# An attention and feed-forward kernel: output product in quadrants, two head chunks in 64x32 tiles, stages from token tables

One core of one Trainium2 chip. The metric is the device time of one execution in microseconds (us), lower is better. Each "time" below is the median of the runs of a kernel; a "span" is that of the one profiled execution and is some 2 us shorter than the time. PE is TensorE and PEld its weight loads, DVE is VectorE, ACT ScalarE, POOL GpSimd; SP is SyncE, whose queue issues transfers. PSUM is the memory that matmuls write.

## The reference

For 8 batches, 12 heads, 448 tokens and head width 64: q and k are normalised by their root mean square, then softmax attention. The result, 3584 rows of 768, goes through a feed-forward layer of width 2048 with a sine in the middle.

```python
q_n, k_n = rmsnorm(q, g_q), rmsnorm(k, g_k)
scores = np.matmul(q_n, k_n.transpose(0, 1, 3, 2)) / np.sqrt(64)
attn = np.exp(scores - max); attn = attn / (sum(attn) + 1e-09)
x = np.matmul(attn, v)                  # -> (B*S, H*D) = (3584, 768)
h = x @ w_in                            # first product, 768 -> 2048
s = np.sin(alpha * h)
g = h + s * s / (alpha + 1e-09)
return g @ w_out                        # output product, 2048 -> 768
```

## The kernel before

The program is unrolled. For each batch there is a stage in which attention runs beside the output product of the batch before; then comes the first product of the batch. I call such a pair a repeat. A batch has three chunks of four heads. `bank_pair` hands out one of four pairs of PSUM banks (a slot): the one that a small clock model, run when the program is built, takes to be free first. The order within a stage comes from a short plan string, between whose entries the output steps and the side work are spaced evenly.

```python
def bank_pair(name, dtype=F32):
    slot = min(free_at, key=free_at.get)          # a modelled time at which each slot comes free
    clock["pe"] = max(clock["pe"], free_at.pop(slot))
    ...

def load_v(b):                                    # four transfers of 64 rows
    ...
    parts = [(slots[pp][key_rows(pp, hi)], tok[hi, pp]) for pp in range(2) for hi in range(2)]
    return [lambda o=o, i=i: nc.gpsimd.dma_start(out=o, in_=i) for o, i in parts]

def load_w_in(half):                              # two transfers of 64 rows a half
    rows = moe_w_in.rearrange("(hi pr d) f -> hi d pr f", hi=2, d=D)
    cols = slice(half * D_FF // 2, (half + 1) * D_FF // 2)
    for hi in range(2):
        nc.gpsimd.dma_start(out=w_in_sb[half][hi * 64:hi * 64 + 64], in_=rows[hi, :, :, cols])

def attend(pi, tiles=range(NJ)):                  # values and 64 copies of the sums, 64x64 tiles
    ...
    nc.tensor.matmul(av[o, part, :S], ones[r, :] if part else vb[b][r, hp, j, :],
                     expT[pi // 2, j][r, pi % 2, :], start=(j == 0), stop=(j == NJ - 1))
    ...

def step(m, unit=unit, st=st):                    # output product, whole array
    ...
    nc.tensor.matmul(st["ps"][:, k, :HALF], g_sb[:, m, c0:c0 + P],
                     w_out_sb[:, m, half * HALF:(half + 1) * HALF], start=(m == 0), stop=(m == MT - 1))
```

In the general stage, the four value loads of the next batch go out one at a time near the end of the attention stage, and the transposes of q and k by DMA (`transpose`, two a chunk, on the SP queue) go out early (those of the batch's own third chunk, which this stage still needs), in the middle and at the end (those of the next batch's first two chunks).

## Time and profile before

| before | |
|---|---|
| time | 436.38 us (436.36 to 437.89) |
| span of the profiled run, mean granted TensorE clock | 434.6 us, 0.996 |
| end of the first product of batch 1, then one repeat | 107.71 us, then 50.35 us each |
| after the last first product (the close) | 24.8 us |

Two more groups of lines of this page: the first lists a DMA queue (packets, MB, share of 16 engines' time); the others an issue (count, KB each, median us from issue to landing).

```profile
q0 software_dynamic: 12416, 11.81, 18.0%
...
w_in<-in_moe_w_in_dram POOLq DMA_DIRECT2D x4, 768.0 KB, 11.9
```

### The profile page before, as it was taken

What the parts mean: (1) busy time and instruction counts of PE and PEld (TensorE: products, weight loads), DVE (VectorE), ACT (ScalarE), POOL (GpSimd) and SP (SyncE); (2) the same over time, 40 slices, a digit from 0 to 9 for tenths busy, and PEclk for the clock granted to TensorE, in tenths of its full rate; (3) what the DMA queues carried; (4) which work ended last, traced back from release to release, by engine and by line L of the source; (5) the groups of instructions that cost most, each with busy time, mean ns of one, the idle gap of its engine ahead of it and who ended that gap; (6) DMA issues with size and microseconds to landing.
All of it is one profiled execution on the core that took longest, in us unless ns stands there. A gap on an engine that the chain in (4) does not pass through costs nothing.

```text
span 434.6 us, 9514 instructions
## 1 busy us (share of the span) xinstructions
PE 423.9 (98%) x3844; PEld 220.5 (51%) x3844; DVE 231.6 (53%) x335; ACT 338.4 (78%) x529; POOL 279.7 (64%) x263
## 2 busy tenths in 40 slices
PE   7889999999999999999999999999999999999996
PEld 3335554555455555555555555555555555555563
DVE  4778564557455564547453564464645474246511
ACT  4889789878888787878879788887878788788600
POOL 4969789936995659927798369947599176002300
PEclk9989999999999999999999999999999999999999
DMA  7999999690249505692067903494063901320022
GB/s 254 209 257 206 215 192 231 143 267 15 67 151 217 144 0 131 121 223 100 10 193 180 194 1 82 150 221 125 1 196 85 126 1 33 84 57 2 0 67 79
DMA packets 68240, 54.63 MB, mean 126 GB/s; under 512 B 39636, under 2 KB 63972, under 8 KB 68196
## 3 DMA queue, kind: packets, MB, share of 16 engines
q1 hardware_dynamic: 54834, 40.51, 36.1%
q0 software_dynamic: 12416, 11.81, 18.0%
q10 hardware_dynamic: 946, 1.70, 1.0%
q8 instruction: 30, 0.49, 0.5%
q14 instruction: 14, 0.11, 0.1%
HBM read 45.62 MB, written 11.01 MB: 130 GB/s over the span
## 4 chain that ended last, share of the span: by engine, by line
PE 82%; DVE 1%; ACT 1%; POOL 0%; issue 0%; POOLq 0%
PE ops L406 32%; PE hps L353 29%; PE av L314 13%; PE sc L294 7%; ACT expT L297 1%; DVE ms L227 0%; POOL sq L221 0%; DVE osb L412 0%; DVE g_sb L340 0%; DVE xT L326 0%; ACT inv L236 0%; ACT inv L237 0%; POOLq L246 0%
## 5 line engine op out<-in xcount | busy, mean ns | idle before, releaser
L297 ACT ACTIVATE expT<-sc 128x896 bf16<-128x896 f32 x168 | 144.7, 914 | 30.6 <-PE sc L294 29.5
L406 PE MATMUL ops<-w_out_sb,g_sb 128*128 128x384 bf16 x896 | 156.6, 327 | 0.0
L353 PE MATMUL hps<-xT,w_in 128*128 128x448 bf16 x768 | 146.8, 353 | 0.0
L335 POOL TENSOR_TENSOR s<-s 128x448 f32<-128x448 f32 x64 | 59.5, 934 | 114.4 <-ACT s L332 100.8
L406 PEld LDWEIGHTS <-g_sb 128*128 128x128 bf16 x896 | 83.1, 98 | 70.0 <-issue 18.8
L340 DVE SCALAR_TENSOR_TENSOR g_sb<-s,inv_alpha_sb,hps 128x448 bf16<-128x448 f32 x128 | 80.8, 676 | 60.9 <-POOL s L335 60.9
L353 PEld LDWEIGHTS <-w_in 128*128 128x128 bf16 x768 | 74.4, 98 | 71.4 <-issue 2.9
L332 ACT ACTIVATE s<-hps,alpha_sb 128x448 f32<-128x448 f32 x128 | 74.6, 628 | 28.3 <-PE hps L353 26.5
L326 DVE TENSOR_TENSOR xT<-av,rec 64x448 bf16<-64x448 f32 x96 | 59.7, 622 | 50.1 <-ACT rec L321 30.8
L246 POOL TENSOR_TENSOR qkn<-qk,inv 128x448 bf16<-128x448 f32 x80 | 72.7, 939 | 7.4 <-POOL qk L224 7.0
L221 POOL TENSOR_TENSOR sq<-qk 128x896 f32<-128x896 f32 x44 | 73.4, 1685 | 0.0
L314 PE MATMUL av<-expT,vb 64*64 64x448 bf16 x672 | 70.6, 352 | 0.6 <-DVE osb L412 0.3
L314 PE MATMUL av<-expT,ones 64*64 64x448 bf16 x672 | 70.7, 352 | 0.0
L227 DVE TENSOR_REDUCE ms<-sq 128x14 f32<-128x896 f32 x44 | 47.5, 1083 | 25.0 <-POOL sq L221 24.7
L412 DVE COPY osb<-ops 128x768 f32<-128x768 f32 (+1 forms) x33 | 27.6, 837 | 51.4 <-PE ops L406 45.5
L294 PE MATMUL sc<-qkT 64*64 64x448 bf16 x672 | 51.3, 362 | 2.5 <-DVE qkT L276 1.4
L224 POOL TENSOR_TENSOR qk<-qk,gg 128x896 f32<-128x896 f32 x24 | 50.2, 2094 | 1.8 <-ACT gg L171 1.8
L314 PEld LDWEIGHTS <-vb 64*64 64x64 bf16 x672 | 37.6, 107 | 12.5 <-issue 1.1
L314 PEld LDWEIGHTS <-ones 64*64 64x64 bf16 x672 | 37.4, 107 | 11.3
L337 ACT ACTIVATE s<-s 128x448 f32<-128x448 f32 x64 | 36.9, 577 | 2.8
L294 PEld LDWEIGHTS <-qkT 64*64 64x64 bf16 x672 | 15.1, 105 | 30.6 <-issue 26.4
L321 ACT ACTIVATE rec<-rec 128x448 f32<-128x448 f32 x48 | 27.7, 577 | 1.5
(44 smaller groups left out, 138.6 us busy)
## 6 DMA issues: line engine op xcount, KB each, us to landing
qk<-in_q_dram SPq DMA_DIRECT2D x24, 448.0 KB, 4.8
qk<-in_k_dram SPq DMA_DIRECT2D x22, 448.0 KB, 4.8
out_dram<-osb SPq DMA_DIRECT2D x39, 192.0 KB, 2.8
vb<-in_v_dram POOLq DMA_DIRECT2D x32, 168.0 KB, 6.4
w_in<-in_moe_w_in_dram POOLq DMA_DIRECT2D x4, 768.0 KB, 11.9
w_out_sb<-in_moe_w_out_dram POOLq DMA_DIRECT2D x2, 1536.0 KB, 24.2
out_dram<-osb SPq DMA_DIRECT2D x26, 96.0 KB, 4.5
qk<-in_k_dram ACTq DMA_DIRECT2D x2, 448.0 KB, 6.0
```

The source lines that it names most:

```text
L221: nc.gpsimd.tensor_mul(st.sq[w], qk[ci][:, w], qk[ci][:, w])
L224: eng.tensor_mul(qk[ci][:, 0], qk[ci][:, 0], gg.to_broadcast([P, 2 * NJ, D]))
L246: eng.tensor_mul(n[:, :, hi, :], x[:, hi], inv[:, hi].unsqueeze(2).to_broadcast([P, NJ, D]))
L294: nc.tensor.matmul(sc[key_rows(pp, hi), pp, :S], qkt[r, 1, j * REST:(j + 1) * REST], qkt[r, 0, :], start=True, stop=True)
L297: nc.scalar.activation(expT[c, j], sc[:, :, :S], ACT.Exp, scale=SCALE)
L314: nc.tensor.matmul(av[o, part, :S], ones[r, :] if part else vb[b][r, hp, j, :], expT[pi // 2, j][r, pi % 2, :], start=(j == 0), stop=(j == ...
L326: nc.vector.tensor_mul(xT[b][r, hp, :], av[r, 0, :S], rec[o, :])
L332: nc.scalar.activation(s1, hps, ACT.Sin, scale=alpha_sb[:, m, :])
L335: nc.gpsimd.tensor_mul(s2, s1, s1)
L340: nc.vector.scalar_tensor_tensor(g_sb[:, m, (b % 2) * S:(b % 2 + 1) * S], s2, inv_alpha_sb[:, m, :], hps, op0=ALU.mult, op1=ALU.add)
L353: nc.tensor.matmul(ps[:, m % 2, :S], w_in_sb[m * 2 // MT][:, kt, m % (MT // 2) * P:(m % (MT // 2) + 1) * P], x[:, kt, :], start=(kt == 0), ...
L406: nc.tensor.matmul(st["ps"][:, k, :HALF], g_sb[:, m, c0:c0 + P], w_out_sb[:, m, half * HALF:(half + 1) * HALF], start=(m == 0), stop=(m == ...
```

## The change

The intent: (1) the output product in four 64x64 quadrants a matmul, so that output, scores and values share one tile shape and TensorE changes shape less often; (2) the sums and values of two of the three head chunks together in eight 64x32 tiles, so that sums are not made twice; (3) the order of a stage written out in tables of tokens instead of spaced evenly from a short plan, with the PSUM slot of each tile named in a string instead of picked by the model. Because the heads are grouped in another way, the loads of values and of the first weights are rewritten as well. Cut to its core (the order code and the first two tables are left out; "..." marks cuts):

```diff
+STAGE_N = (
+    (
+        "r2 S 1 q40 5 f f f k20 f 1 S 3 f 1 f u40 S S f 1 k21 1 q41 q31 1 t2 S 1 V1 1 S 1 g4 1 S 2 u31 S "
+        "1 u41 S 2 S f f 1 S 2 S 2 q30 S 1 S o6 o1 v4 1 v1 u30 S v1 g3 r4 v1 f f 1 k41 2 S 1 S 1 l5 1 f "
+        "q50 S f k40 f S f 1 q51 t4 S 1 r3 1 k30 1 k31 S 1 x1 l6 x6 y4 y1 y2 z2 z2 z2 z1 "
+    ),
+    "32103020210230230310310132131313103210210",
+    {-1: 'g5 t3', 0: 'u50', 5: 'u51', 6: 'l7'},
+)
+LAST = "0123012"
...
     def bank_pair(name, dtype=F32):
-        slot = min(free_at, key=free_at.get)
-        clock["pe"] = max(clock["pe"], free_at.pop(slot))
+        slot = int(upcoming.popleft())
+        free_at.remove(slot)
...
     def load_v(b):
-        parts = [(slots[pp][key_rows(pp, hi)], tok[hi, pp]) for pp in range(2) for hi in range(2)]
-        return [lambda o=o, i=i: nc.gpsimd.dma_start(out=o, in_=i) for o, i in parts]
+        heads = v[b].rearrange("(g pp) (p j) d -> (pp p) g (j d)", pp=2, j=NJ)
+        nc.gpsimd.dma_start(out=vb[b].rearrange("p g j d -> p g (j d)"), in_=heads)
...
     def load_w_in(half):
-        rows = moe_w_in.rearrange("(hi pr d) f -> hi d pr f", hi=2, d=D)
         cols = slice(half * D_FF // 2, (half + 1) * D_FF // 2)
+        pairs = moe_w_in.rearrange("(c hi pp d) f -> c pp hi d f", c=NC, pp=2, d=D)
+        quarters = moe_w_in.rearrange("(g x d) f -> g x d f", x=2, d=D // 2)
+        for pp in range(2):
+            nc.gpsimd.dma_start(out=w_in_sb[half][:, pp], in_=pairs[0, pp, :, :, cols])
+        for x in range(2):
+            nc.gpsimd.dma_start(out=w_in_sb[half][:, 2 + x], in_=quarters[4:8, x, :, cols])
         for hi in range(2):
-            nc.gpsimd.dma_start(out=w_in_sb[half][hi * 64:hi * 64 + 64], in_=rows[hi, :, :, cols])
+            for pp in range(2):
+                g = 8 + 2 * hi + pp
+                nc.gpsimd.dma_start(out=w_in_sb[half][strip(2, pp, hi), 4:6], in_=quarters[g, :, :, cols].rearrange("x d f -> d x f"))
...
+            for hi in range(2):
+                for c in ((1, 2) if both else (0,)):
+                    for pp in range(2):
+                        r = slice(pp * 64, pp * 64 + 64)
+                        o, k = (strip(c, pp, hi), c - 1) if both else (slice(hi * 64, hi * 64 + 64), pp)
+                        d = slice(D // 2) if kind in ("ones", "low") and both else slice(D // 2, D) if both else slice(D)
+                        w = ones[r, d] if kind == "ones" else vb[b][r, 2 * c + hi, j, d]
+                        nc.tensor.matmul(av[o, k, :S], w, expT[b * NC + c, j][r, hi, :], start=(j == 0), stop=(j == NJ - 1))
...
+            def quadrants(m, unit=unit, st=st):
...
+                for r in range(2):
+                    for o in range(2):
+                        rs, os = slice(r * 64, r * 64 + 64), slice(o * 64, o * 64 + 64)
+                        nc.tensor.matmul(st["ps"][os, r, :HALF], g_sb[rs, m, c0 + o * 64:c0 + o * 64 + 64],
+                                         w_out_sb[rs, m, half * HALF:(half + 1) * HALF], start=(m == 0), stop=(m == MT - 1))
+                if m == MT - 1:
...
+                    nc.vector.tensor_copy(osb[:, 0], st["ps"][:, 0, :HALF])
+                    nc.vector.tensor_add(osb[:, 0], osb[:, 0], st["ps"][:, 1, :HALF])
...
+            step = whole_array if b == B - 1 else quadrants
```

In the tables, a number is so many output steps, S a chunk of scores, o v x y z the sums and values, t a pair of DMA transposes, V the load of values, W and O the first and the output weights; the string of digits names the slot of each PSUM tile in turn.

## The prediction

> **What bounds the kernel now.** I read the page's busy shares and the 40 slices first, then the chain that ended last in order of time over one whole repeat, then the groups by shape, the waits, and the busy time by stage.
>
> ```profile
> span 434.6 us, 9514 instructions
> PE 423.9 (98%) x3844; PEld 220.5 (51%) x3844; DVE 231.6 (53%) x335; ACT 338.4 (78%) x529; POOL 279.7 (64%) x263
> PE   7889999999999999999999999999999999999996
> DMA  7999999690249505692067903494063901320022
> ```
>
> PE is at 98%, but matmul ends are modelled and matmuls overlap, so the share alone proves little. The chain does prove it. From 81 us on it is PE alone until the last copy, and every repeat (one batch: attention beside the output product of the batch before, then the first product) takes the same 50.35 us: first product ends at 107.71, 158.06, 208.41, 258.76, 309.12, 359.47, 409.82. Inside one repeat:
>
> ```profile
> 158.06 1.95 PE ops L406 x12
> 160.01 0.50 PE sc L294 x8
> 160.51 2.38 PE ops L406 x14
> 162.89 0.50 PE sc L294 x8
> ...
> 169.87 2.71 PE ops L406 x16
> 172.57 0.50 PE sc L294 x8
> 173.07 1.32 PE av L314 x28
> 174.40 0.19 PE sc L294 x4
> 174.59 2.38 PE ops L406 x14
> ...
> 186.17 3.97 PE av L314 x84
> 190.14 18.27 PE hps L353 x96
> ...
> 409.82 20.81 PE ops L406 x128
> ```
>
> Columns: start in us, length in us, engine, tile and line, matmuls. I read unit prices out of it:
> - Whole-array output product (384 columns): the closing 128 matmuls take 20.81, or 162.6 ns each.
> - 64x64 tiles (448 columns): 84 value and sum matmuls take 3.97, or 189 ns for each four. Four quadrants truly run at once; I call four a round. A chunk of scores is one round, 0.19.
> - First product: 18.27/96 = 190 ns each, or 189 ns plus one entry of about 0.11.
> - **The price of changing tile shape.** 14 output matmuls after scores take 2.38, but 14 x 0.1626 = 2.28; 8 scores after output take 0.50, but two rounds are 0.38. So each change between 128x128 and 64x64 costs 0.10 to 0.12 us. Where the shape stays (first product to output: 12 in 1.95; scores to values: 28 in 1.32), nothing is added.
>
> The repeat from 158.06 has 18 such changes. Check of the sum: 112 output matmuls 18.21, first product 18.16, 21 scores 3.97, 42 rounds of values and sums 7.94, which is 48.28; the other 2.07 over 18 changes is 0.115 each. No part of the repeat is a wait.
>
> ```profile
> L406 PE MATMUL ops<-w_out_sb,g_sb 128*128 128x384 bf16 x896 | 156.6, 327 | 0.0
> L314 PE MATMUL av<-expT,vb 64*64 64x448 bf16 x672 | 70.6, 352 | 0.6 <-DVE osb L412 0.3
> L314 PE MATMUL av<-expT,ones 64*64 64x448 bf16 x672 | 70.7, 352 | 0.0
> ```
>
> The means of 327 and 352 ns are latencies, not prices. Half the attention product, 672 matmuls, only makes sums of the exponentials, copied to 64 rows each. ACT is busy 27.4 of the 32.1 us of the attention stage and 14.3 of 18.3 beside the first product; POOL 26.9 and 9.7; DVE 15.8 and 11.4. All have room, ACT and POOL the least.
>
> **What the Trainium skill says.**
> - "TensorEngine Tiling (Array Packing)", Key Properties: a change of tiling mode, not just of tile, drains TensorE. The trace agrees, at 0.115 us a change.
> - Same page, Available Configurations and Key Properties: 64x32 mode has eight tiles, and different tiles load weights and multiply in parallel. The trace confirms it for four 64x64 tiles (189 ns a round, eight score weight loads begun in about 35 ns); no 64x32 tile occurs in it.
> - Same page, Restrictions: column tiling turns Fast Weight Load off. In the trace a 64x64 load takes 106 ns against 98 for a full one; four together still hide under a round.
> - Same page, Gotcha 1 (PSUM Pressure): different row tiles may not be in one PSUM bank at once. Hence a quadrant product must leave two half sums in two banks, and DVE must add them. Nothing in the trace contradicts it; before never has two row tiles in the same bank and rows.
>
> **The change part by part.**
> 1. *Output product in quadrants* (all batches but the last). One matmul becomes four of 64x64. By the price of a round I expect the same 162.6 ns: no gain in arithmetic, 768 matmuls become 3072. The gain is that output, scores and values now share one shape. In the general plan the shape changes only at first product to output, into the 64x32 tiles at the end, and out of them into the first product: 3 changes for 18. That is 15 x 0.115 = 1.7 us a batch. The stage of batch 1 has 5 for 18: 1.5 us.
> 2. *Two chunks together in 64x32 tiles.* One chunk alone still takes 14 rounds (7 of sums, 7 of values). The other two took 28; now sums, low half and high half take 7 each, eight matmuls a round, because one set of sums 32 rows high serves both value halves. 42 rounds become 35: 7 x 0.189 = 1.3 us a batch, if eight tiles overlap as four do. Starts about 5 ns apart leave room for sixteen instructions inside 189 ns.
> 3. *What moves off PE.* ACT: twelve Ln and Exp a batch at 0.55 to 0.58 become four of 896 columns at about 0.9: 6.7 becomes 3.7 us. DVE: twelve products of 64x448 at 0.622 (7.5 us) become three of 128x896 at about 1.0 (3 us). But each half output row now costs a copy of 0.56 and an add I put at 0.6 (estimate: the copy of the same size): about 8 us instead of 4. DVE is about even, at 28 of 47 us. None of this is on the path; it takes ACT load off a stage that shrinks by 3 us.
> 4. *Loads.* Values come in one transfer instead of four (saves POOL about 2 us of issue a batch at 0.64 each); the first weights come in eight instead of two per half (some 4 us more POOL issue for each half, once, in the opening stage). Bytes are unchanged.
> 5. *Opening stage* (to 39.67). It also saves 7 rounds and about 3 us of ACT, but its DMA share is 0.94, POOL is 29.6 of 39.7 busy, and PE waits there for transposes and scaling. I count 1.0 us.
> 6. *Close.* The last batch's output keeps its whole-array form: the 24.8 us after 409.82 stay.
>
> **Sum.** Six repeats (batches 2 to 7) at 1.7 + 1.3 = 3.0: 18.1 us. Batch 1: 1.5 + 1.3 = 2.8, and about 0.5 of the 1.2 us of waiting that its stage has now (48.94 against 47.7 of work): 3.3. Opening: 1.0. Together 22.4 off. I give back 0.6 for new small waits on named slots and half sums. 436.4 - 22.4 + 0.6 = **414.4 us**; each repeat should read 47.3 us.
>
> **Rivals.**
> - *Eight tiles do not overlap fully.* If a 64x32 round cost 25% more (twice the instructions to place), 21 rounds x 0.047 = 1.0 us a batch: about 422. If it ran as two rounds of four, the 21 cost 4.0 us a batch more, some 32 us in eight batches, and the change would lose. For: no such tile was ever timed here. Against: load starts about 5 ns apart.
> - *The quadrants are bound by their weight loads.* A round of 384 columns is 27 ns shorter than the 448 ones whose loads are seen to hide. If a quadrant round also cost 189 ns, 112 x 0.026 = 2.9 us a batch, some 20 us over the seven batches: about 434, no gain. Against: two batches of loads, eight in all, fit into 0.14 us.
> - *ACT becomes the bound.* After the first product ends it still has 1.8 us of sines and squares, 1.28 of table load, then 21 exponentials at 0.83 back to back, 3.7 of reciprocals and 1.6 of norms: about 26 in a stage of 29. It fits, but a bad order would show as PE waiting on expT: up to 1 us a batch, about 421.
> - *The opening stays bound by transfers.* The slices show DMA at 90% and more up to about 65 us; an earlier PE then waits for weights: the 1.0 and part of batch 1 fall away, about 417.
>
> **Range and chances.** The middle rests on measured prices; what can go wrong adds time, except that the reordered opening may save 2 or 3 us instead of 1. So 410 to 420. Only a failure of concurrency, not a wait, could bring it within 2% (above 427.7): 0.95 faster, 0.04 within, 0.01 slower.
>
> **What would show each step right or wrong.** In the chain: first-product ends 47.3 us apart (46.8 to 48); scores after output at 0.19 a round with no added 0.12; output at 0.65 us for sixteen quadrant matmuls; 56 matmuls of a 64x32 part in 1.32 us. In the waits: the 80 idle gaps "issue" ahead of score weight loads (26.4 us in all) nearly gone. DVE about where it is now, ACT some 20 us lower. Wrong if output rounds read over 0.17 us, if the 64x32 parts read over 1.4 us, or if PE waits on expT, half-sum adds or weights for more than 5 us outside the first 20 us.

## More of the kernel before

The view of DMA issues over the whole run has, for the 40 transposes:

```profile
qkT<-qkn SPq DMA_TRANSPOSE x40, 4.1
```

## The result, and the profile after

The changed kernel takes **465.89 us** (464.3 to 473.32, four runs, of which the longest is slow) against 436.37 (434.85 to 437.89): the ratio is 1.0675, 95% interval 1.0631 to 1.0719. Ratios here are the mean time of one kernel's fast runs over that of the other's fast runs of the same rounds, so not quite the ratio of the medians. Without its slow run the median of the changed kernel is 465.23 us, and that of e1 459.58 for 460.72; the differences from the changed kernel given below would then be 0.7 us smaller, e1's 0.5 us larger. The kernel is 6.8% slower where I had predicted 5% faster. Its results are correct.

The page of the kernel after. The rows of digits are 40 slices of the span:

```profile
span 463.5 us, 14846 instructions
...
PE 413.9 (89%) x6598; PEld 245.6 (53%) x6598; DVE 225.8 (49%) x331; ACT 316.3 (68%) x465; POOL 275.1 (59%) x251
...
PE   4988099878996999979998999979997999999796
...
PEclk9999689998998899989999999989999999999899
...
q0 software_dynamic: 17344, 11.83, 19.0%
...
w_in<-in_moe_w_in_dram POOLq DMA_DIRECT2D x8, 256.0 KB, 16.7
w_in<-in_moe_w_in_dram POOLq DMA_DIRECT2D x8, 128.0 KB, 16.6
```

PE has 10 us less to do than before, as intended, and yet the span is 29 us longer. PE now has holes (the 0 in the fifth slice, the 6s and 7s), and the granted clock falls at the longer holes. The software queue q0 moves the same megabytes in 4,928 packets more, and the first weights land later in pieces of 256 KB than they did in pieces of 768 KB.

The chain of work that ended last, in order of time (start, length, what):

```profile
36.27 15.95 DMA w_in<-in_moe_w_in_dram
...
102.17 3.91 issue
106.09 1.30 PE av L352 x16
107.39 19.08 PE hps L392 x96
...
282.68 3.58 PE ops L471 x88
...
292.78 0.33 PE ops L471 x8
293.29 10.59 DMA qkT<-qkn
303.93 0.58 PE sc L326 x2
...
312.83 4.10 PE av L352 x168
316.92 18.27 PE hps L392 x96
...
437.04 22.46 PE ops L452 x128
```

The unit prices are the predicted ones: 88 quadrant matmuls in 3.58 us are 162.7 ns for four, and 168 of the 64x32 matmuls in 4.10 us are 195 ns for eight. But a DMA transpose of 10.59 us now stands in the chain of a repeat, a weight transfer of 16 us in the opening, and the closing product takes 22.46 us where it took 20.81. The waits say the same (total us, times, longest), first those of PE:

```profile
PE sc L326 <- DMA qkT<-qkn: 15.9, 6, 4.3
PE hps L392 <- DVE qkn L281: 12.1, 1, 12.1
PE aps L204 <- DMA small<-in_moe_alpha_dram: 6.0, 1, 6.0
PE av L352 <- issue: 4.6, 3, 3.9
PE ops L452 <- DVE g_sb L378: 3.1, 1, 3.1
```

In the profile before, the longest wait of PE with a named cause was 1.4 us in three pieces. Behind the 12.1 us stands POOL, which took its work in the order of the program:

```profile
POOL w_out_sb L227 <- DMA w_in<-in_moe_w_in_dram: 9.8, 1, 9.8
```

POOL could not issue the output weights before a first-weight transfer had landed. Behind that issue stands the product that folds in the norm's weights, then the scaling (`qkn`) on DVE, and that holds the PSUM slot which the first product was to take.

By stage, with the predicted span taken as 414.4 less the 1.8 us by which the time before exceeds its span:

| us | before | predicted | after | after less predicted |
|---|---|---|---|---|
| end of the first product of batch 1 | 107.7 | 103.4 | 126.5 | +23 |
| six repeats after it | 302.1 | 283.8 | 307.5 | +24 |
| close | 24.8 | 24.8 | 29.5 | +5 |
| span | 434.6 | 412.6 | 463.5 | +51 |

The predicted stages add up to 412.0; the rest is the 0.6 us that I gave back without a place.

### The profile page after: what moved, and what is told of

Read it like the earlier page. It is cut to its first block, busy times and chain, and to the rows that moved or that the text cites. A ratio compares the mean times of both kernels' runs of the same rounds, so it can differ in the third digit from the quotient of the medians.

```text
span 463.5 us, 14846 instructions
## 1 busy us (share of the span) xinstructions
PE 413.9 (89%) x6598; PEld 245.6 (53%) x6598; DVE 225.8 (49%) x331; ACT 316.3 (68%) x465; POOL 275.1 (59%) x251
## 4 chain that ended last, share of the span: by engine, by line
PE 71%; DMA 21%; POOL 3%; issue 2%; ACT 2%; DVE 1%; POOLq 0%; SPq 0%; ACTq 0%
PE hps L392 28%; PE ops L471 21%; DMA qkT<-qkn 14%; PE av L352 8%; PE sc L326 6%; PE ops L452 5%; DMA w_in<-in_moe_w_in_dram 3%; DMA qk<-in_k_dram 3%; PE ps L234 2%; DMA small<-in_moe_alpha_dram 1%; POOL qk L259 1%; POOL sq L256 1%; ACT s L370 1%; ACT expT L329 1%; POOL w_out_sb L227 1%
## 5 line engine op out<-in xcount | busy, mean ns | idle before, releaser
L392 PE MATMUL hps<-xT,w_in 128*128 128x448 bf16 x768 | 149.8, 356 | 13.1 <-DVE qkn L281 12.1
L471 PE MATMUL ops<-w_out_sb,g_sb 64*64 64x384 bf16 x3072 | 154.6, 329 | 0.5 <-issue 0.5
L471 PEld LDWEIGHTS <-g_sb 64*64 64x64 bf16 x3072 | 99.7, 109 | 38.4 <-issue 2.1
L326 PE MATMUL sc<-qkT 64*64 64x448 bf16 x672 | 68.5, 356 | 17.8 <-DMA qkT<-qkn 15.9
L364 DVE TENSOR_TENSOR xT<-av,rec 128x896 bf16<-128x896 f32 x24 | 25.6, 1089 | 57.0 <-PE av L352 38.9
L477 DVE COPY osb<-ops 128x384 f32<-128x384 f32 x48 | 26.7, 557 | 50.7 <-PE ops L471 50.7
L352 PE MATMUL av<-expT,vb 64*32 64x448 bf16 (+1 forms) x1120 | 41.8, 358 | 4.6 <-issue 4.6
L352 PEld LDWEIGHTS <-vb 64*32 64x32 bf16 (+1 forms) x1120 | 21.1, 97 | 16.5 <-issue 7.2
L478 DVE TENSOR_TENSOR osb<-osb,ops 128x384 f32<-128x384 f32 x48 | 26.6, 554 | 1.7
L352 PE MATMUL av<-expT,ones 64*32 64x448 bf16 (+1 forms) x672 | 25.3, 350 | 0.0
L452 PE MATMUL ops<-w_out_sb,g_sb 128*128 128x384 bf16 x128 | 22.4, 341 | 3.1 <-DVE g_sb L378 3.1
## 6 DMA issues: line engine op xcount, KB each, us to landing
w_in<-in_moe_w_in_dram POOLq DMA_DIRECT2D x8, 128.0 KB, 16.6
```

What stands on the lines that cost most here:

```text
L326: nc.tensor.matmul(sc[pp * 64:pp * 64 + 64, hi, :S], qkt[r, 1, j * REST:(j + 1) * REST], qkt[r, 0, :], start=True, stop=True)
L352: nc.tensor.matmul(av[o, k, :S], w, expT[b * NC + c, j][r, hi, :], start=(j == 0), stop=(j == NJ - 1))
L392: nc.tensor.matmul(ps[:, m % 2, :S], w_in_sb[m * 2 // MT][:, kt, m % (MT // 2) * P:(m % (MT // 2) + 1) * P], x[:, kt, :], start=(kt == ORD ...
L471: nc.tensor.matmul(st["ps"][os, r, :HALF], g_sb[rs, m, c0 + o * 64:c0 + o * 64 + 64], w_out_sb[rs, m, half * HALF:(half + 1) * HALF], star ...
```

## The experiments

Thirteen kernels ran: twelve timed, and one look after them, for what was still open. Each expectation stands as it was recorded before the run.

**e1: other closing slots.** The last eight first-product tiles take slots 0, 3, 2, 1, 0, 2, 1, 0, so the closing product, which begins with slot 0 by the table, begins with the slot that is released last.

```diff
-LAST = "0123012"
+LAST = "3210321"
```

> The changed kernel with only the closing list of PSUM slots renamed from 0123012 to 3210321, so that the first unit of the last output product takes the slot that came free first and not the one that the last snake tile still holds. Theory (named slot): the 3.1 us wait of PE on g_sb at 434 us and the half-clock stretch behind it go; the closing 128 matmuls take 20.8 us again instead of 22.5; about 4.7 us less, near 461. Rival (the last snake tile itself is late, whatever the slot): no change.

Measured 460.72 us (one of its four runs was slow), 1.055 of before [1.0499, 1.0602], so 5 us under the changed kernel. The chain shows the close as it was before:

```profile
412.56 18.27 PE hps L392 x96
430.83 20.81 PE ops L452 x128
```

The wait of 3.1 us is gone and so is the half-clock stretch that followed it. This cause is settled.

**e2: the values load later.** In the table of the general stage, `V1` follows just behind `t2`, the two transposes of the third chunk.

```diff
-... 1 t2 S 1 V1 1 S 1 g4 ...        -... k31 S 1 x1 l6 x6 ...
+... 1 t2 S 1 1 S 1 g4 ...           +... k31 S 1 V1 x1 l6 x6 ...
```

> The changed kernel with the load of the next batch's values moved from just behind the DMA transposes of the third chunk to the end of the attention stage. Theory (the 1.4 MB load slows the transposes): PE's waits on the transposes in the repeats (15.0 us) and the half-clock stretches after them go, repeats fall from 50 to 54 us to about 48, as in the last repeat, which has no such load; 10 to 19 us less, near 450. Rival (the transposes are late because scaling on POOL ends late or because the SP queue holds them): under 3 us.

Measured 441.99 us, 1.0142 [1.0117, 1.0167]: 24 us off, more than the 10 to 19 expected, and enough alone to account for the repeats. They now take 47.3 to 48.3 us. The issues of the stretch from 335 to 360 us in the kernel after, where both transposes of the third chunk and the value load fall (KB each where given, median us to landing):

```profile
vb<-in_v_dram POOLq DMA_DIRECT2D x1, 672.0 KB, 10.0
...
qkT<-qkn SPq DMA_TRANSPOSE x2, 6.7
```

The same batch's third chunk in e2 (326 to 330 us), with no value load beside it:

```profile
qkT<-qkn SPq DMA_TRANSPOSE x2, 3.4
```

PE waits for the slower of a pair: in the kernel after it was issued at 346.1 us and took 10.01 us. But e2 has only moved the load to another pair. There it runs beside the transposes of the next batch's second chunk (300 to 306 us):

```profile
vb<-in_v_dram POOLq DMA_DIRECT2D x1, 672.0 KB, 11.5
...
qkT<-qkn SPq DMA_TRANSPOSE x2, 10.3
```

These are slowed as much, and PE doesn't wait, because it needs them only 26 us after the first was issued (301.2, first use 327.2). The third chunk's pair is needed some 8 us after its issue (326.7, 334.7). In the kernel before it is the same: the transposes beside value loads take 4.7 to 8.4 us, those of the third chunk, ahead of the loads, some 3.3. So what cost the time is not that a load slows transposes, but that it was put beside the one pair that is needed soon.

The expectation was too small because it counted the waits, 15.0 us in the repeats, and too little for the clock after them: the mean granted clock from 126 to 434 us is 0.98, some 6 us in all; from 144.7 to 194.9 us it is only 0.93.

**e3: four weight transfers fewer.** The last third of the first weights goes into a tile of its own that serves both halves, 12 transfers for 16. The idea then was that the number of transfers did the harm: the program's semaphores for this queue go round in eight, so a transfer waits for the one eight places ahead of it.

```diff
+    w_last = wpool.tile([P, 2, D_FF], BF16, name="w_last")
...
+        if half:
+            return
...
-    ...out=w_in_sb[half][strip(2, pp, hi), 4:6], in_=quarters[g, :, :, cols]...
+    ...out=w_last[strip(2, pp, hi)], in_=quarters[g]...
...
```

> The changed kernel with the weights of the first product in 12 transfers instead of 16 (the rows of the last third for both halves at once). Same bytes, same place in the order. Theory (eight transfer semaphores in rotation: the first output weights wait for the first transfer of the second half to land, POOL stands still for 9.8 us, the fold behind it keeps a PSUM slot): POOL's wait ahead of the output weights goes from 9.8 to under 2 us, PE's wait of 12.1 us in the first product of batch 0 goes, the first product of batch 1 ends at 110 to 116 instead of 126 us; 10 to 16 us less. The first half is 1 MB larger, which may cost up to 4 us at its start. Rival (the bytes cannot come sooner): within 3 us of the changed kernel.

Measured 457.07 us, 1.0491 [1.044, 1.0541]: 9 us off, just under the expected range. The first product of batch 1 still ends at 120.7 us, 17 us after the predicted place, so most of the opening's loss was something else.

**e4: e1, e2 and e3 together.**

> The three edits together. If the three causes are separate, the gains add: 465.9 - 4.7 - 15 - 13, near 433, about the kernel before; repeats near 48 us. If they hide one another, the sum is clearly less than the three alone.

Measured 432.03 us, 0.9926 [0.9876, 0.9975]. From batch 2 on the predicted 47.3 us comes true, at 47.31:

```profile
99.96 18.27 PE hps L396 x96
...
147.27 18.27 PE hps L396 x96
...
194.58 18.27 PE hps L396 x96
```

Four of the six repeats take 47.31 us; the two others, 48.20 and 47.93, have each one of the halts in them that e13 is about. Over all six the granted clock is 1.00.

**e5: e4 with the whole-array output product.** This asks whether the quadrants are worth their instructions, in the order of tokens that the change has.

```diff
-            step = whole_array if b == B - 1 else quadrants
+            step = whole_array
```

> The kernel of e4 (three schedule edits) with the output product of every batch in whole 128x128 matmuls again; the order of all steps stays. In that order the tile shape then changes 42 times in a general repeat instead of 3, and 33 instead of 5 in batch 1. Theory (a change of shape costs 0.115 us): 6 x 39 x 0.115 + 28 x 0.115 = 30 us more than e4, repeats near 51.8 us. Rival (changes are hidden here, the quadrants bring nothing): within 3 us of e4; DVE is freed of the 48 adds in any case.

Measured 456.52 us, 1.05 [1.0469, 1.0531]: 24.5 us more than e4, against an expected 30. In the groups by line, the loads of weights for scores and output now wait longer without a named cause (in e4 "issue" stands at 8.2 us for scores and 1.3 for the quadrants; here busy us, mean ns, then idle us before them and what ended it):

```profile
L456 PEld LDWEIGHTS <-g_sb 128*128 128x128 bf16 x896 | 76.7, 98 | 70.8 <-issue 30.0
...
L329 PEld LDWEIGHTS <-qkT 64*64 64x64 bf16 x672 | 18.6, 103 | 48.1 <-issue 46.7
```

Each repeat has 42 changes of shape in this order for 3 with quadrants. In the profiled runs the six repeats take 312.3 us for e4's 285.4: 26.9 us over 6 x 39 = 234 changes, or 0.115 us each, the price read from the kernel before. What is missing from the 30 is in batch 1, whose repeat is 2.4 us shorter than e4's (48.3 for 50.7) where 3.2 more were expected.

**e6: the kernel before with eight weight transfers a half.** If it is the number of transfers that costs, the kernel before must suffer from it too. All have 64 rows.

```diff
-            nc.gpsimd.dma_start(out=w_in_sb[half][hi * 64:hi * 64 + 64], in_=rows[hi, :, :, cols])
+            for pr in (slice(0, 2), slice(2, 4), slice(4, 5), slice(5, 6)):
+                nc.gpsimd.dma_start(out=w_in_sb[half][hi * 64:hi * 64 + 64, pr], in_=rows[hi, :, pr, cols])
```

> The kernel before with each half of the first weights in eight transfers instead of two; same bytes, same layout, same place in the order. Theory (eight semaphores in rotation): the output weights again wait for the first transfer of the second half, POOL stands still there for 5 us or more, and the time rises by 4 to 15 us. Rival (the opening of the changed kernel is bound by other things, such as its own order): within 2 us of before.

Measured 440.43 us, 1.0134 [1.0104, 1.0164]. It is 5.5 us slower, but by another route than expected: POOL spends 6.2 us instead of 1.3 on issuing the first half (1.8 of it waiting for value loads to land), and what stands behind comes later. There is no wait ahead of the output weights, and the pieces land early, in some 8 us. The same number of transfers as in the changed kernel therefore lands in half the time. My theory of the number fell here as the main cause; what the number costs is these 5.5 us.

What differs is in the packets. In the changed kernel the trace has 5,552 packets of 4 bytes on the software queue, in e6 816, in before 624. I took it then for the form of eight of the sixteen transfers: 128 rows that lie at two strides in memory.

**e7: the kernel before with quadrants alone.**

```diff
...
+                for r in range(2):
+                    for o in range(2):
+                        rs, os = slice(r * 64, r * 64 + 64), slice(o * 64, o * 64 + 64)
+                        nc.tensor.matmul(st["ps"][os, r, :HALF], g_sb[rs, m, c0 + o * 64:c0 + o * 64 + 64], ...)
...
+                    nc.vector.tensor_copy(osb[:, 0], st["ps"][:, 0, :HALF])
+                    nc.vector.tensor_add(osb[:, 0], osb[:, 0], st["ps"][:, 1, :HALF])
```

> The kernel before with nothing changed but its output product in quadrants (all batches but the last), with half sums added on DVE. Theory: 16 of 18 changes of shape a batch go: 7 x 16 x 0.115 = 12.9 us less, near 423, repeats near 48.5 us. Rival (new waits on slots and half sums eat it): 430 or more.

Measured 434.2 us, 0.9975 [0.9954, 0.9996]. The changes of shape fall from 18 to 2 a batch as meant, but repeats fall only from 50.35 to 49.63 us, not to 48.5, and that of batch 1 grows from 48.8 to 51.8. PE now waits for DVE, which has two passes a half row and is not placed for it in this order:

```profile
PE sc L294 <- DVE osb L446: 3.9, 8, 1.4
```

These named waits are less than what is missing, and 2.5 us of them fall in batch 1; the rest wasn't followed. In this order, then, the quadrants brought little; in the order of the change (e5 against e4) they brought 24.5 us.

**e8: a first attempt at the best version.** The edits of e1 and e2, seven weight transfers a half by another assignment of strips, and a reordered opening.

```diff
...
+        for x in range(2):
+            nc.gpsimd.dma_start(out=w_in_sb[half][:96, 4 + x], in_=quarters[9:12, x, :, cols])
+        nc.gpsimd.dma_start(out=w_in_sb[half][96:, 4:6], in_=quarters[8, :, :, cols].rearrange("x d f -> d x f"))
```

> The changed kernel with the late value load and the renamed closing slots, and a mended opening: the blank matmuls first on PE, the first weights in seven transfers a half (another choice of strips), issued 2 us earlier, the fold of the next batch's first chunk ahead of them on POOL, the second half of the output weights and the values later. Theory (the opening is all that is left): POOL no longer stands ahead of the output weights; first product of batch 1 ends near 105 instead of 118 us in e4; near 418, range 414 to 424. Rival (transfers bind the opening): above 426.

Measured 432.34 us, 0.994 [0.9913, 0.9966]: a clear miss, 14 us over, in the range of the rival. Fewer transfers, and yet 7,184 packets of 4 bytes; PE waited 8.7 us for first weights. So e9 went the other way, to more transfers.

**e9: ten transfers a half, none of more than 64 rows.** With the edits of e1 and e2.

```diff
...
+        rows = moe_w_in.rearrange("(g x d) f -> g d x f", x=2, d=D // 2)
+        pairs = moe_w_in.rearrange("(c hi pp d) f -> c hi d pp f", c=NC, pp=2, d=D)
+        for hi in range(2):
+            nc.gpsimd.dma_start(out=w[hi * 64:hi * 64 + 64, 0:2], in_=pairs[0, hi, :, :, cols])
+        for c in (1, 2):
+            for hi in range(2):
+                for pp in range(2):
+                    nc.gpsimd.dma_start(out=w[strip(c, pp, hi), 2 * c:2 * c + 2], in_=rows[4 * c + 2 * hi + pp, :, :, cols])
```

> The changed kernel with the late value load and the renamed closing slots (as in e4), and the first weights in ten transfers a half, each of at most 64 rows that lie at one stride in DRAM, in place of e4's twelve in all. More transfers than in the changed kernel (8), same bytes. New theory (not the number of transfers but their form: those of 128 rows at two strides carry some 640 packets of 4 bytes each, 5120 in all, and their data starts 6 us after the issue): packets of 4 bytes fall from 5488 to about 500, the first weights land before 37 us, the first product of batch 1 ends near 112 instead of 118 us; 422 to 427. Rival (number of transfers and the eight semaphores): the opening is no better than that of the changed kernel, 436 or more.

Measured 425.23 us, 0.978 [0.9746, 0.9814], as expected (whether it is over 2% is unclear). There are 496 packets of 4 bytes, and the first product of batch 1 ends at 112.66 us.

```profile
q0 software_dynamic: 12288, 11.81, 18.6%
...
w_in<-in_moe_w_in_dram POOLq DMA_DIRECT2D x16, 128.0 KB, 7.2
w_in<-in_moe_w_in_dram POOLq DMA_DIRECT2D x4, 256.0 KB, 5.4
```

**e10: e9 with the opening's order mended.** The sines' factors no longer lead on PE, and blank matmuls keep it busy from the start; other tokens and slots of the opening moved too, as the expectation says.

```diff
-        "q01 L q00 u01 G u00 g0 r01 k01 q10 r00 b11 u10 q11 k00 b15 g1 u11 ...
+        "b11 q01 q00 u01 G u00 g0 r01 k01 q10 r00 u10 q11 k00 b15 g1 u11 ...
...
```

> e9 with the opening order mended as well: blank matmuls first on PE, the product for alpha after the first scores, the fold of the next batch's first chunk ahead of the second half of the weights, second half of the output weights and the next values inside the first product. Theory: scores start at 12 us instead of 17, the first product of batch 0 near 37 and that of batch 1 ends near 106; 413 to 420. Rival (transfers bind the opening): equal to e9 within 2 us.

Measured 423.72 us, 0.975 [0.9712, 0.9788]. The rival, no gain beyond 2 us over e9, was the nearer one: the gap at the start is closed, but the third chunk's norms now come late (PE waits 3.4 us for one transposed copy). It is the fastest of the timed kernels, 2.5% under before.

**e11: the kernel before with six transfers a half of 128 rows.** The mirror of e9: it puts the suspected form, and less of the number, into the kernel before.

```diff
-        for hi in range(2):
-            nc.gpsimd.dma_start(out=w_in_sb[half][hi * 64:hi * 64 + 64], in_=rows[hi, :, :, cols])
+        for pr in range(6):
+            nc.gpsimd.dma_start(out=w_in_sb[half][:, pr], in_=rows[:, :, pr, cols])
```

> The kernel before, with each half of the first weights in six transfers of 128 rows at two strides (one per row of tiles) in place of two of 64 rows. Theory (the form of a transfer, 128 rows at two strides, costs, not the number of transfers): each of the twelve carries 640 packets of 4 bytes, about 7,700 in all against 624 before; the weights land late, and the kernel is slower than the one with eight transfers of 64 rows a half (440.4) although it has fewer transfers: 444 us or more, with the first product of the first batch waiting for weights. Rival (each transfer costs its issue and its lane, whatever its form): six transfers cost less than eight, so 437 to 440 us and no more 4-byte packets than before.

Measured 448.84 us, 1.0323 [1.0272, 1.0375]: 14 us slower than before and 8 slower than e6, with four transfers fewer. The form costs more than the number. The lines of its page:

```profile
q0 software_dynamic: 23296, 11.85, 19.3%
...
w_in<-in_moe_w_in_dram POOLq DMA_DIRECT2D x12, 256.0 KB, 18.4
```

But there were 11,504 packets of 4 bytes and not 7,700: my 640 a transfer was wrong, and working out why gives a likely mechanism. The Trainium skill, "DMA: Bandwidth & Descriptors", section "Why a DMA increments its semaphore by 16 and not by 1", says that a transfer is spread over k of the 16 DMA engines, k being the largest number up to 16 that divides the slowest dimension (of more than one element) of both its patterns, and that on the software queue all 16 post a completion, whatever the shape. `rows[:, :, pr, cols]` begins with a dimension of two, so k is 2. Suppose that each idle engine is given one packet of 4 bytes for every row that a working engine moves, and each engine one more at the end. Then a transfer has 16 + (16 - k) x rows / k of them:

| transfer (rows, slowest dimension) | k | 4-byte packets |
|---|---|---|
| 64 rows, or 128 as one dimension | 16 | 16 |
| 128 rows as 2 x 64 (`pairs`; all of e11's) | 2 | 16 + 14 x 64 = 912 |
| 128 rows as 4 x 32 (`quarters`) | 4 | 16 + 12 x 32 = 400 |
| 96 rows as 3 x 32 (e8) | 3 | 16 + 13 x 32 = 432 |

| kernel | worked out: weights + the rest | counted in the trace |
|---|---|---|
| before | 4 x 16 + 560 | 624 |
| e6 | 16 x 16 + 560 | 816 |
| e11 | 12 x 912 + 560 | 11504 |
| e9 | 20 x 16 + 176 | 496 |
| after | 4 x 912 + 4 x 400 + 8 x 16 + 176 | 5552 |
| e8 | 4 x 912 + 4 x 400 + 4 x 432 + 2 x 16 + 176 | 7184 |

The rest is 16 for each of the 35 and 11 other transfers of this queue. The sum is right to the packet in all six (and in e3, with four transfers of 16 packets fewer: 5,488). The trace doesn't tell which engine carried a packet, so that the data went through two or four engines, and the small packets to the others, is inferred from the counts and the page's rule. By it a 256 KB transfer of the changed kernel had two or four of the sixteen engines. Whether the few engines or the small packets cost the time, no run separates. Nor does a slow transfer delay itself alone: the pieces of 128 KB at k = 16 that stand behind it in the changed kernel landed as late, after 16.6 us.

**e12: the changed kernel with e9's transfers alone.** The same test in the changed kernel.

> The changed kernel with one thing changed: each half of the first weights in ten transfers of at most 64 rows at one stride, in place of eight of which four have 128 rows at two strides. The early value load and the closing slots stay as they are. Theory (the form of these transfers is what delays the opening by some 14 us): the first product of the second batch ends at 111 to 115 instead of 126.5, its later repeats stay at 50 to 54 us each, time 450 to 454 us. Rival (the reordered opening itself, its tokens and slots, costs the time): the first product of the second batch ends at 120 or later, time 459 or more.

Measured 447.45 us, 1.0297 [1.0235, 1.0358]. The first product of batch 1 ends at 112.56 us, 14 us earlier, as expected, and its repeats keep 48 to 54 us. The time is 18.4 us under the changed kernel, 3 us better than the range. The form of the weight transfers is the cause of 14 of the 23 us that the opening lost.

**e13: more blank matmuls (one look).** In the kernel after, and likewise in e4, e9, e10 and e12, PE halts in three places (in some also in a few others) for which the profile names no wait ("issue"), after matmuls 1243, 3803 and 6363 of the kernel after: 2,560 matmuls, with their loads 5,120 instructions, from one to the next. In the profile of e10 these are 1240, 3800 and 6360; it has six event instructions more.

```diff
-            keep_busy(int(token[1:]), blank)
+            keep_busy(4 * int(token[1:]), blank[:, :128])
```

> The best version so far, with the 26 blank matmuls of the opening, of 512 columns each, cut into 104 of 128 columns: the same TensorE time, 78 matmuls more ahead of all the work. Theory (TensorE stops when it has gone through so many instructions, 5,120 from one stop to the next, as if the next stretch of the program had to come in): the stops stay at matmuls no. 1240, 3800 and 6360, which is now work that stood 78 matmuls earlier. Rival (the stops belong to a place in the work, whatever the count): they move to no. 1318, 3878 and 6438. Time within 1 us of 423.7 in both.

Neither came out. The halts are now after matmuls 3028 and 5588, again 2,560 apart, and at none of the six places named (a single run of unknown state, 422.19 us). Less the 78 new matmuls, 3028 is 1710 on from 1240, and two repeats have 2 x 852 = 1704, so the halt came at the same place of another repeat, in the 64x32 part, where the most instructions pass in a us.

The traces say more. Each page counts packets on an instruction queue, first the kernel after, then the kernel before:

```profile
q8 instruction: 51, 0.84, 0.8%
...
q8 instruction: 30, 0.49, 0.5%
```

Each packet has 16,384 bytes, and there is one for every 256 instructions of TensorE (13,210 and 7,698 in the two traces). Over all kept traces PE has 42 halts of 0.25 us or more without a named cause. Counted in instructions (matmuls, loads and events, with what a trace lost added), 38 of them lie whole multiples of 256 apart, and each of the 38 ends 1.2 to 1.6 us after such a packet has landed. This also explains the distance: 5,120 is twenty blocks of 256, and three repeats have 5,112 instructions, so every third repeat a block begins at nearly the same place of the 64x32 part. The halts thus fit instructions that arrive too late. No run tests it.

## Why the prediction was wrong

**What was right: the mechanism and its prices.** Part 1, a round of four quadrants at 162.6 ns: measured 162.7. Part 2, 64x32 rounds as fast as 64x64: 195 ns for eight against 189 for four, 3% more. Part 3: ACT 22 us lower (predicted some 20), DVE 6 us lower (about even), the add of half sums 554 ns (0.6), the product of 128x896 1,089 ns (1.0). "Each repeat should read 47.3 us" is what e4 shows. None of the rivals on eight tiles, on quadrants' weight loads or on ACT came true. The last sum of the prediction has a slip, 436.4 - 22.4 + 0.6 is 414.6; nothing hangs on it.

**The step that failed: "I give back 0.6 for new small waits on named slots and half sums."** It stands for everything that the new order could do to other work, and I had not read the order at all. It measured as three separate terms, together 51 us:

1. *The order of transfers in a repeat: +24 us.* I had looked at DVE, ACT and POOL in the shrunken stage, and at the issue cost of the values' load ("saves POOL about 2 us of issue"), but not at when it goes out and beside what. Behind `t2` it is under way at the same time as the one pair of transposes that PE needs within 8 us; one took 10.6 us where the third chunk's take 3.4 without the load. e2 takes the wait away with one token, by moving the load beside a pair that is needed later.
2. *Part 4, "Bytes are unchanged", and part 5, "I count 1.0 us".* The bytes were unchanged, the spread over DMA engines was not. +23 us at the end of the first product of batch 1: 14 by the form of the weights' transfers (e12), 9 remaining. Of those, e10 gets back less than 1 (111.9 us against 112.66). My fourth rival named the place, an opening bound by transfers, but gave it 3 us, for it supposed the transfers to be as fast as before.
3. *Part 6, "the 24.8 us after 409.82 stay": +5 us.* "Stay" was right of the arithmetic and wrong of its slot. The order of slots was in the diff, one line, and by the tables could have been checked against the last eight tiles. e1 settles it.

The waits also cost clock: the closing wait was 3.1 us, and the product after it lost 1.65 more at half clock. The signs of being wrong that I had named (PE waiting on expT, half sums or weights) did not catch this: the waits were on transposes, on scaled copies behind POOL and on the last `g_sb`.

**The range.** "Only a failure of concurrency, not a wait, could bring it within 2%" was wrong by its form: it took the small waits of one order to mean that any order has small waits. The change replaced the even spacing and the slot model by tables; so the absence of waits before was no evidence for after, and the chance of slower should have been well over 0.01.

**What stays open.** The single repairs take off 5.2, 23.9 and 18.4 us, 47.5 in sum, but together (e9) 40.7. By stage they do add up: 4.7 in the close (e1), 22.1 in the six repeats (e2) and 13.9 in the opening (e12) make 40.7. The surplus of the single runs lies in stages that their edits don't touch and varies between runs: in e1 the first product of batch 1 ended 2.7 us earlier than in the changed kernel, and e12's four runs spread over 5.5 us. Between e10 and the predicted 414.4 us lie 9 us. In the stages, 8.5 are in the opening (111.9 against 103.4), where one order was mended and another wait came up, and 1.7 in the six repeats, 47.6 us each for 47.3, less the 0.6 given back. All of the 1.7 is in the two repeats with a halt (48.2 and 48.1 us; the other four take 47.31).

## What to carry to other kernels

When a change rewrites the order of work, the unit prices tell what the best order would give, and not what this order gives: go through the new order for each transfer, and ask what will be in flight beside it, who waits for that, and how soon. Read the access patterns of a load that was rewritten, not only its bytes: put a dimension first that 16 divides, and count the packets of the queue afterwards. Where a table names buffers, check the first of each stage against the last of the stage before.

## What the Trainium skill lacked or had wrong

- "DMA: Bandwidth & Descriptors", section "Why a DMA increments its semaphore by 16 and not by 1": its rule for k fits all six packet counts here. It lacks the packets of 4 bytes that come with a small k on this queue (by the counts here one to each idle engine for each row that a working engine moves: 896 beside the 16 completions at k = 2) and what a small k costs: 256 KB land in 18.4 us at k = 2 (e11), and in 7.9 (e6) or 5.4 (e9) at k = 16, all medians from issue to landing with other transfers under way.
- The same page: no figure for a DMA transpose beside a load. Here pairs under way with a load of 672 KB had medians of 6.7 (the changed kernel) and 10.3 us (e2), against 3.4 for a pair without it (e2).
- "TensorEngine Tiling (Array Packing)": no price for the drain at a change of tiling mode (0.115 us in the kernel before, and again from e5's repeats), and none for a round of eight 64x32 tiles of 448 columns (195 ns).
- "Runtime: NRT & Kernel Launch", section "Instruction fetch mechanics": it has blocks of 256 instructions, which the trace agrees with (one packet of 16,384 bytes for every 256 instructions of TensorE), and the cost of crossing into the next as mostly hidden. Here 38 halts of TensorE of 0.25 to 3.9 us lie at such crossings, in ten of the fifteen kernels. Whether late blocks cause them no run here tests.
